# Moving the block for the expected head pattern out of a conditional, and the block for other patterns behind it

## The chip, the core and the metric

The kernel runs on one core of one Trainium2 chip. Its five engines work from queues of their own, in order, and meet at semaphores: TensorE (PE, matrix products; PEld stands for its weight loads), VectorE (DVE), ScalarE (ACT), GpSimd (POOL) and SyncE (SP), which here only issues transfers. The metric is the device time of one execution in microseconds.

## The reference

Two stages follow each other. The first is attention over 4 batches, 8 heads, 768 positions and 64 values per head; some heads ("retrieval") see all earlier positions, the others only 4 first positions and a window of 64:

```python
scores = scale * np.matmul(q, k.transpose(0, 1, 3, 2))
stream_keep = causal & (is_sink | in_win)
mask = np.where(retr[0, :, 0, 0, None, None], full_mask, stream_mask)
scores = np.where(mask[None, :, :, :], scores, -1000000000.0)
a = softmax(scores)              # written out in the original
x = np.matmul(a, v)              # heads joined: 4 x 768 x 512
```

The second is a gated circular convolution along the 768 positions, done with Fourier transforms:

```python
x1, x2, x3 = split(x @ w_proj, 3)
x2_conv = np.fft.irfft(np.fft.rfft(x2, axis=1) * np.fft.rfft(filter_fft, axis=0), n=S, axis=1)
out = (x1 * x2_conv * x3) @ w_out
```

Which heads are retrieval heads is an input, `is_retrieval`; it is 1, 0, 1, 0, 0, 0, 1, 0.

## The kernel before, in words

The kernel holds two complete programs for this. `patterned` is laid out for the expected pattern of heads and leaves out the blocks that the mask makes empty; `general` works for any pattern. Which one runs is decided on the chip: `lflag` (L1016) loads `is_retrieval`, four VectorE instructions (L1027 to L1030) compare it with the pattern and leave 0 or 1 in the tile `other`, every engine loads that value into a register (L1788) and branches on it (L1789).

Inside `patterned` every step is a named operation, and two strings of names give the order in which they are recorded. `AHEAD` is run before the branch, `FAST` in its else-block. A recording layer then gives each engine its queue; it works on one straight stretch of code at a time, and a branch ends a stretch. So in this kernel the instructions of `AHEAD` stand ahead of the branch on every engine and those of `FAST` behind it.

`AHEAD` holds: the load of the flag and of the first q and k blocks (`lflag lk0 lq0 lk1 lq1`, L1016, L1369); the comparison; and the start of the Fourier tables. The tables come out of a short chain: `tfrac` (L1080, VectorE), `turns` (L1133, ScalarE), then `angle`, `wrap`, `size` (L1137, L1141, L1146, VectorE), then `sin` and `cos` (L1151, L1155, ScalarE). Beside it `mtab0` and `mtab1` (L1096, VectorE, and L1100, GpSimd) start the mask table, and five matrix products on zeros (`blank0`, L1041) give TensorE something to do.

`FAST` begins with what the first attention blocks need. `ck0`, `cq0` (L971, VectorE) turn the loaded k and q to 16 bits; `T0.1`, `T0.0` (L1407) transpose them on TensorE; `E0.1`, `E0.0` (L971 on VectorE, L975 on ScalarE) copy the transposes out; `sc` (L1452) makes scores; `sb` (L1465) adds the mask as a product of the identity with a table `btab`; `ex` (L1471, ScalarE) takes the exponential. `btab` (L1129, VectorE) waits for the rest of the mask table, `mtab2` and `mtab3` (L1107 to L1125, GpSimd). Beside it the Fourier tables are finished from sine and cosine: `skew0` and `skew1` (L1163 on ScalarE, L1161 on GpSimd), the `G` tiles (L1161, L1188, L1201, L973), and `Gh` (L1214, VectorE). Later, per batch, come the projections (L1655, L1620), the spectra (L1620 to L1638), the inverse transform (L1685) and the output product (L1712), which is stored from L1732 and L1734.

The two blocks of the conditional lie one behind the other in the code of each engine, `FAST` first. An engine that ends `FAST` jumps over the whole of `general` (3517 instructions on PE) to a common end. There SP waits in turn for all transfers and all engines, the last for the last store, and then a barrier of all engines ends the program.

Of the kernel before, what the change touches and what calls it, by code (L numbers as in the profile page):

```python
# [9 lines left out]
FP32 = mybir.dt.float32  # L10
# [110 lines left out]
AHEAD = """  # L121
# [1632 lines left out]
@with_exitstack  # L1754
def kernel(
    ctx: ExitStack,
    tc: tile.TileContext,
    q: bass.AP,
    k: bass.AP,
    v: bass.AP,  # L1760
    is_retrieval: bass.AP,
    n_sink: bass.AP,
    window: bass.AP,
    moe_w_proj: bass.AP,
    moe_filter_fft: bass.AP,
    moe_w_out: bass.AP,
    out: bass.AP,
):
    nc = tc.nc
    H = q.shape[1]  # L1770
    assert H == 8 and int(window) <= 64 and int(n_sink) <= 64
    first = ctx.enter_context(tc.tile_pool(name="first", bufs=1))
    raw = {name: first.tile([128, size // 2], BF16, name="r_" + name) for name, size in RAW.items()}
    pools = {"raw": raw}
    raw["P0"] = raw["P"][:, 0:768]
    raw["P1"] = raw["P"][:, 768:2304]
    for name, size in (("mtab", 1792), ("other", 4), ("flag", 64), ("zeros", 64), ("local", 32), ("want", 32),
                       ("differs", 32)):
        raw[name] = first.tile([128, size // 2], BF16, name="r_" + name)
    run, held, left = patterned(tc, pools, None, q, k, v, is_retrieval, int(n_sink), int(window), moe_w_proj,  # L1780
                                moe_filter_fft, moe_w_out, out)
    engine = mybir.EngineType
    engines = {engine.Pool, engine.SP, engine.DVE, engine.PE, engine.Activation}
    with tc.tile_pool(name="bpsum", bufs=1, space=bass.MemoryType.PSUM) as psum:
        pools["space"] = psum.tile([128, 8, 512], FP32, name="bspace")
        with tc.manual_schedule(engines=engines):
            run(AHEAD)
    reg = nc.values_load(held["other"][0:1, 0:1], min_val=0, max_val=1)  # L1788
    with tc.If(reg != 0, preferred_fallthrough_block=False) as cmp:  # L1789
        general(tc, raw, q, k, v, is_retrieval, n_sink, window, moe_w_proj, moe_filter_fft, moe_w_out, out)  # L1790
    with cmp.Else(), ExitStack() as inner:
        inner.enter_context(tc.manual_schedule(engines=engines))
        pools["sb"] = inner.enter_context(tc.tile_pool(name="fsb", bufs=1))
        psum = inner.enter_context(tc.tile_pool(name="fpsum", bufs=1, space=bass.MemoryType.PSUM))
        pools["space"] = psum.tile([128, 8, 512], FP32, name="space")
        run(FAST)
    assert not left(), left()


# [33 lines left out]
```

## Time and profile before

| | |
|---|---|
| median of 3 runs | 190.54 us (190.18 to 191.35) |
| the profiled execution's own time | 190.34 us |
| its span in the profile | 188.6 us, so 1.74 us lie outside it |
| granted TensorE clock, mean | 0.985 |
| busy: PE, DVE, ACT, POOL | 176.5, 161.1, 145.7, 68.5 us |
| issues of the branch (L1789), first and last | POOL 3.6 us, SP 4.1, DVE 4.6, ACT 5.1; at the end ACT 182.6, SP 183.7 |

The span begins with the first instruction of the program and ends with its last barrier. An engine's busy time counts only work, not branches, register loads, waits or the issue of transfers; those show in the views of a line or of the waits. The chain of waits follows the work that ended last back to the start, from each piece to what released it.

### The profile page before, as it was taken

The page shows a single profiled execution, that of the slowest core. Times are in us where ns is not written, and L with a number is a line of the kernel's source. Part 1 is how long each engine was busy: PE and PEld are TensorE (multiplying, and loading weights), DVE is VectorE, ACT ScalarE, POOL GpSimd, SP SyncE. Part 2 cuts the span into 40 slices and gives each one's busy share as a digit, 9 for nine tenths or more (in the row PEclk, how much of TensorE's full clock was granted, in tenths as well). Part 3 has the DMA queues.
Part 4 walks back from the last instruction along what each step waited for, and adds up shares of the span by engine and source line. Part 5 has one row for each costly group of instructions (what it writes and reads, how often), then busy time and mean ns, then how long its engine had stood idle before and what let it go on. Part 6 is the DMA issues. An engine that isn't in the chain of part 4 may idle for free.

```text
span 188.6 us, 4479 instructions
## 1 busy us (share of the span) xinstructions
PE 176.5 (94%) x1694; PEld 103.5 (55%) x1694; DVE 161.1 (85%) x329; ACT 145.7 (77%) x210; POOL 68.5 (36%) x103
## 2 busy tenths in 40 slices
PE   6989999989998999999999999999999999999970
PEld 2446664647745563575555656655657765455420
DVE  6886799889979999999979999999899996499810
ACT  5887899999999999988989999696976331435350
POOL 5884785554322224570250450600741630000000
PEclk9988999999999999999999999999999999999997
DMA  4999999999999999999999989922262002412083
GB/s 161 332 270 283 206 196 239 271 292 240 219 198 229 210 210 171 218 220 194 231 244 254 217 250 225 214 47 50 82 76 111 3 2 113 146 24 111 37 299 126
DMA packets 78960, 34.06 MB, mean 181 GB/s; under 512 B 68306, under 2 KB 75218, under 8 KB 78930
## 3 DMA queue, kind: packets, MB, share of 16 engines
q1 hardware_dynamic: 75986, 30.81, 72.8%
q0 software_dynamic: 2944, 2.88, 9.1%
q8 instruction: 15, 0.25, 0.6%
q14 instruction: 15, 0.12, 0.3%
HBM read 24.64 MB, written 6.29 MB: 164 GB/s over the span
## 4 chain that ended last, share of the span: by engine, by line
PE 67%; ACT 14%; DVE 11%; issue 3%; POOL 2%; DVEq 0%; ACTq 0%; POOLq 0%
PE space L1655 19%; PE space L1712 11%; PE space L1620 8%; PE space L1452 7%; PE space L1685 7%; PE space L1516 6%; ACT f_pT L1471 5%; ACT f_HAB L1274 3%; PE space L1465 2%; PE space L1569 2%; DVE f_attn L1533 1%; PE space L1571 1%; ACT f_xh L975 1%; DVE r_P L978 1%; PE space L1407 1%
## 5 line engine op out<-in xcount | busy, mean ns | idle before, releaser
L1471 ACT ACTIVATE f_pT<-space 128x1024 bf16<-128x1024 f32 (+3 forms) x68 | 58.8, 917 | 6.3 <-PE space L1465 2.1
L1655 PE MATMUL space<-f_xT,f_wproj 128*128 128x384 bf16 x256 | 47.9, 326 | 0.1
L1655 PEld LDWEIGHTS <-f_wproj 128*128 128x128 bf16 x256 | 24.0, 98 | 17.0 <-issue 1.0
L1712 PE MATMUL space<-f_wout,r_gy 128*128 128x512 bf16 x96 | 24.7, 379 | 0.0
L1452 PE MATMUL space<-f_qkT 64*128 64x128 bf16 (+3 forms) x248 | 22.4, 252 | 1.2 <-DVE f_qkT L971 0.6
L1620 PE MATMUL space<-f_wproj,f_xh 128*128 128x512 bf16 x96 | 22.7, 379 | 0.1
L1685 PE MATMUL space<-f_Gi,r_P 128*128 128x384 bf16 x96 | 19.1, 326 | 0.6 <-ACT f_evs L975 0.3
L978 DVE TENSOR_TENSOR f_pT<-f_pT,r_mtab 128x1024 bf16<-128x1024 bf16 (+3 forms) x33 | 18.5, 585 | 1.0 <-ACT f_pT L1471 0.8
L975 ACT COPY f_o<-space 128x1024 f32<-128x1024 f32 (+1 forms) x12 | 9.9, 836 | 11.3 <-PE space L1712 11.2
L1516 PEld LDWEIGHTS <-f_pT 128*128 128x128 bf16 x472 | 16.6, 97 | 3.6 <-issue 0.9
L1516 PE MATMUL space<-f_v_aug,f_pT 128*128 128x65 bf16 x392 | 17.9, 193 | 0.6 <-ACT f_X L975 0.5
L978 POOL TENSOR_TENSOR f_uv<-f_fo 128x256 bf16<-128x256 bf16 x12 | 9.1, 765 | 23.3 <-DVE f_fo L978 19.0
L1452 PEld LDWEIGHTS <-f_qkT 64*128 64x128 bf16 x248 | 10.3, 94 | 13.1 <-issue 10.4
L1696 DVE TENSOR_TENSOR f_conv<-f_evs,space 128x384 bf16<-128x384 f32 x32 | 16.1, 547 | 0.6 <-PE space L1685 0.3
L975 ACT CAST f_xh<-space 128x768 bf16<-128x768 f32 x14 | 11.2, 808 | 4.9 <-PE space L1573 4.6
L1620 PEld LDWEIGHTS <-f_xh 128*128 128x128 bf16 x96 | 9.0, 97 | 10.0 <-issue 0.4
L1712 PEld LDWEIGHTS <-r_gy 128*128 128x128 bf16 x96 | 9.0, 98 | 8.9 <-issue 0.4
L1533 DVE TENSOR_TENSOR f_attn<-space,f_rec 128x768 bf16<-128x768 f32 x14 | 13.4, 955 | 0.4
L1685 PEld LDWEIGHTS <-r_P 128*128 128x128 bf16 x96 | 8.8, 97 | 7.3 <-DVE r_P L978 0.9
L978 POOL TENSOR_TENSOR f_fo<-f_attn 128x384 bf16<-128x384 bf16 x11 | 10.4, 957 | 2.4 <-DVE f_attn L1533 1.9
L975 ACT CAST f_X<-space 128x1024 bf16<-128x1024 f32 x8 | 8.2, 1019 | 2.8 <-PE space L1620 2.0
L978 POOL TENSOR_TENSOR f_pT<-f_pT,r_mtab 128x512 bf16<-128x512 bf16 (+1 forms) x6 | 6.7, 1117 | 9.5 <-ACT f_pT L1471 9.5
(136 smaller groups left out, 346.2 us busy)
## 6 DMA issues: line engine op xcount, KB each, us to landing
f_v_f<-in_v_dram SPq DMA_DIRECT2D x32, 192.0 KB, 4.8
out_dram<-f_o SPq DMA_DIRECT2D x9, 512.0 KB, 2.9
r_qk_f<-in_k_dram SPq DMA_DIRECT2D x10, 192.0 KB, 4.5
r_qk_f<-in_q_dram SPq DMA_DIRECT2D x10, 192.0 KB, 5.3
r_qk_f<-in_k_dram SPq DMA_DIRECT2D x4, 384.0 KB, 11.4
r_qk_f<-in_q_dram SPq DMA_DIRECT2D x4, 384.0 KB, 6.0
f_qk_f<-in_q_dram SPq DMA_DIRECT2D x4, 384.0 KB, 5.5
f_qk_f<-in_k_dram SPq DMA_DIRECT2D x4, 384.0 KB, 6.6
```

The costliest lines, as they stand in the source:

```text
L975: nc.scalar.copy(out=out, in_=in_)
L978: (nc.gpsimd if now["engine"] == "p" else nc.vector).tensor_tensor(out, a, b, op)
L1274: nc.scalar.activation(out=out_(), in_=in_(), func=AF.Copy, scale=w / S)
L1452: nc.tensor.matmul(sc[:, bank, col:col + 128 * cnt], lhsT=keys, rhs=qkT(n)[rows, 0, 128 * i:128 * (i + cnt)], start=(col == 0 or not biase ...
L1471: nc.scalar.activation(out=pT(n)[:, c, :, 0:w], in_=held[f"sc.{n}.{c}"][:, :, 0:w], func=AF.Exp, scale=SCALE)
L1516: nc.tensor.matmul(att[:, hh, 65 * i:65 * i + 65], lhsT=pT(n)[:, c, bank, col:col + 128], rhs=values, start=(z == 0), stop=(z == len(here) ...
L1533: nc.vector.tensor_mul(attn(n).rearrange("p i hh d -> p hh i d"), rows[:, :, :, 0:64], held[f"rec.{n}"][:, :, :, None].to_broadcast([128, ...
L1620: nc.tensor.matmul(ps[:, u, :], lhsT=xh(b)[:, cc, chain, 128 * part:128 * part + 128], rhs=wproj()[:, cc, DM:2 * DM], start=(cc == 0), sto ...
L1655: nc.tensor.matmul(ps[:, s, 0:HS], lhsT=wproj()[:, cc, part * DM + cb * 128:part * DM + (cb + 1) * 128], rhs=xT(b)[:, cc, s * HS:s * HS + HS],
L1685: nc.tensor.matmul(ps[:, 0, 0:HS], lhsT=P(b)[:, t, u, ch], rhs=Gi()[:, tile_no], start=(m == 0), stop=(m == 2))
L1696: fn(conv[:, half * HS:half * HS + HS], held[f"evs.{b}.{cb}"], held[f"c_ps.{b}.{cb}.1"][:, 0, 0:HS])
L1712: nc.tensor.matmul(ps, lhsT=gy(b)[:, cb, i * 128:(i + 1) * 128], rhs=wout()[:, cb, :], start=(cb == 0), stop=(cb == NC - 1))
```

## The change

`patterned`'s two parts now both stand in the straight code, ahead of the conditional; the test is done behind them; and only if the pattern is another one, `AHEAD` is run once more and then `general`, which overwrites the output. A hint at the very first instruction of every engine names the branch and says that it is likely taken (past the block).

```diff
-    run, held, left = patterned(tc, pools, None, q, k, v, ...)
+    def prepared():
+        return patterned(tc, pools, None, q, k, v, ...)
...
+    def ahead(run, name):
+        with tc.tile_pool(name=name, bufs=1, space=bass.MemoryType.PSUM) as psum:
+            pools["space"] = psum.tile([128, 8, 512], FP32, name="bspace")
+            with tc.manual_schedule(engines=engines):
+                run(AHEAD)
+
+    run, held, left = prepared()
+    tc.mark_branch_hint_location("other", "LikelyTaken", engines)
+    ahead(run, "bpsum")
     reg = nc.values_load(held["other"][0:1, 0:1], min_val=0, max_val=1)
-    with tc.If(reg != 0, preferred_fallthrough_block=False) as cmp:
-        general(tc, raw, q, k, v, ...)
-    with cmp.Else(), ExitStack() as inner:
+    with ExitStack() as inner:
         inner.enter_context(tc.manual_schedule(engines=engines))
...
         run(FAST)
     assert not left(), left()
+    with tc.If(reg != 0, label="other"):
+        ahead(prepared()[0], "apsum")
+        general(tc, raw, q, k, v, ...)
```

In the built program `AHEAD` and `FAST` are now one stretch, and the recording layer orders them as one. Past the first twenty instructions every engine's queue is what it was, up to the end. The start of VectorE's queue, before and after, by the names used above (`copy E0.1` is the copy out of the first transpose):

```
before: blank want table        tfrac quarter mtab0 zeros            local            differs reduce angle wrap size | branch | ck0 par cq0 copy-E0.1 | Gm00 btab ck1 Gm01 Gh0 ...
after:  blank want table   ck0  tfrac quarter mtab0 zeros  par  cq0  local copy-E0.1  differs reduce angle wrap size |                              | Gm00 btab ck1 Gm01 Gh0 ...
```

(`zeros`, `local`, `differs`, `reduce` are the four instructions that compare the flags.) `ck0` waits for the first load of k, `cq0` for that of q, the copy for the transposes. On GpSimd two memsets (L1353) stand ahead of L1089 and L1100, and L1120 to L1125 follow as before. ScalarE and TensorE keep their order and lose the load and the branch. SP issues the next transfers without the branch and loads `other` behind its tenth transfer; the other engines load it at the very end.

At the end each engine loads `other`, branches, and lands in a small block of its own, again past the whole of the other block. It holds what brings the semaphores to the same values that the other way would leave: on SP eight waits, one for each of the eight semaphores of transfers, the last of them for the last store. Behind it stands the common end as before, with SP's twelve waits and the barrier.

More of the change, by code (lines that the diff above doesn't have):

```diff
@@ L1779 @@
         raw[name] = first.tile([128, size // 2], BF16, name="r_" + name)
-    run, held, left = patterned(tc, pools, None, q, k, v, is_retrieval, int(n_sink), int(window), moe_w_proj,
-                                moe_filter_fft, moe_w_out, out)
+    def prepared():
+        return patterned(tc, pools, None, q, k, v, is_retrieval, int(n_sink), int(window), moe_w_proj,
+                         moe_filter_fft, moe_w_out, out)
     engine = mybir.EngineType
     engines = {engine.Pool, engine.SP, engine.DVE, engine.PE, engine.Activation}
[L1784 to L1787, printed above, removed]
+    def ahead(run, name):
[6 more added lines that the diff above has]
+    ahead(run, "bpsum")
     reg = nc.values_load(held["other"][0:1, 0:1], min_val=0, max_val=1)
-    with tc.If(reg != 0, preferred_fallthrough_block=False) as cmp:
-        general(tc, raw, q, k, v, is_retrieval, n_sink, window, moe_w_proj, moe_filter_fft, moe_w_out, out)
-    with cmp.Else(), ExitStack() as inner:
+    with ExitStack() as inner:
         inner.enter_context(tc.manual_schedule(engines=engines))
@@ L1797 @@
     assert not left(), left()
+    with tc.If(reg != 0, label="other"):
+        ahead(prepared()[0], "apsum")
+        general(tc, raw, q, k, v, is_retrieval, n_sink, window, moe_w_proj, moe_filter_fft, moe_w_out, out)
 _INS = ['q', 'k', 'v', 'is_retrieval', 'n_sink', 'window', 'moe_w_proj', 'moe_filter_fft', 'moe_w_out']
```

## The prediction

> **What bounds the kernel now.** I read the chain of waits first: on the page as shares, then piece by piece for the first 32 us, because the change touches the start.
>
> ```profile
> ## 4 chain that ended last, share of the span: by engine, by line
> PE 67%; ACT 14%; DVE 11%; issue 3%; POOL 2%; DVEq 0%; ACTq 0%; POOLq 0%
> ```
>
> No transfer is in it: what ends last is a chain of engine work from start to end, two thirds of it TensorE. Its first pieces (start us, us, what):
>
> ```profile
> 3.42 0.57 DVE r_gy L1141
> ...
> 4.01 0.57 DVE r_gy L1146
> ...
> 4.61 0.62 ACT r_P L1155
> ...
> 5.31 1.06 POOL f_skew L1161
> ...
> 7.17 0.52 POOL r_mtab L1113
> ...
> 7.78 1.04 POOL r_G L1161
> ...
> 9.29 0.67 DVE f_Gh L1214
> ...
> 11.03 0.88 DVE f_qkT L971
> ...
> 11.95 0.37 PE space L1452
> 12.32 0.53 PE space L1465 x4
> ```
>
> So the sine and cosine are on the path: `wrap`, `size`, `cos`, then GpSimd without a gap (skew, mask, G), VectorE without a gap from 9.29, scores at 11.95. Behind that each piece starts where the one before it ends. What delays 11.95 by some time delays the end by that time, as long as the pieces behind it keep their lengths. The register load and the branch are not in the chain: GpSimd has done with them at 3.6 us and waits for `cos` until 5.31.
>
> Then the branch's own line (min/median/max ns, first to last start us):
>
> ```profile
> L1789 PEldq COMPARE_BRANCH  x2: 90/2256/4422, 3.6 to 178.6; - x2
> L1789 SPq COMPARE_BRANCH  x2: 46/48/49, 4.1 to 183.7; - x2
> L1789 ACTq COMPARE_BRANCH  x2: 38/42/45, 5.1 to 182.6; - x2
> ```
>
> The branch at the start costs each engine 0.05 to 0.1 us behind a register load of 0.47 to 0.54 us (L1788). The jump at the end is far: 4.42 us on PE itself; on ScalarE the first instruction behind it (L1828) comes at 185.8, 3.2 us after the jump at 182.6; on VectorE 3.0.
>
> Last, the clock in stretches (length; PE, PEld, DVE, ACT, POOL busy with counts; PE clock, DMA share, GB/s):
>
> ```profile
> 8.90:12.30 3.40, 2.31 (x23) 0.99 (x22) 3.13 (x8) 3.07 (x4) 2.57 (x9) 1.00 1.18 299
> 12.30:15.70 3.40, 3.40 (x24) 2.21 (x24) 1.76 (x3) 3.03 (x4) 3.37 (x7) 0.50 1.29 227
> 15.70:19.10 3.40, 3.40 (x46) 2.30 (x44) 2.78 (x5) 2.03 (x3) 0.68 (x3) 1.00 1.01 324
> ```
>
> A stretch with PE busy 2.31 of 3.40 us is followed by one at half the clock.
>
> **1. The start: VectorE's new order (+5.2 us).** The removed branch saves nothing on the chain. But `ck0` now stands ahead of `tfrac`, and `par`, `cq0` and the copy of the transposes ahead of `angle`; a queue is in order, so the sine waits for the first load of k. I walk the queue with start-to-start steps from the timeline of the profile.
>
> - The first k block is issued at 1.23 and takes 3.2 us to land (the shortest of L1369's first landings): 4.4. SP's queue is the same up to there. `ck0` starts at 4.45 (0.05 from landing to start, as for GpSimd's cast at 10.93 after a landing at 10.88).
> - `ck0` to the next 0.52, `tfrac` to `quarter` 0.09, `quarter` to `mtab0` 0.19, `mtab0` to `zeros` 0.73, `zeros` to `par` 0.09, `par` to `cq0` 0.16, `cq0` to the next 0.62, `local` to the copy 0.13: the copy starts at 6.98. TensorE's transposes, released by `ck0` at 5.05, need 0.5 us: not late.
> - copy to the next 0.87, `differs` 0.19, `reduce` 0.08: `angle` at 8.12, against 2.90 now. Then 0.52 to `wrap`, 0.59 to `size`, 0.60 to `cos` at 9.83, 0.62 its length: 10.45, against 5.23.
>
> The chain goes on behind `cos` with the queues that it had: GpSimd's skew at 10.5, its last mask instruction to 12.9, `btab` behind that, G, `Gh`, the copy. VectorE's four pulled-up instructions are done, but it has nothing to do until ScalarE's skew at 10.9, and from `Gh` on it is released by GpSimd again. So 11.95 becomes 17.2: **+5.2**. ScalarE is shifted a little less: it follows `cos` with 0.4 + 0.5 + 1.28 + 0.2 + 0.4 us (skew, G, table load, two small ones), no longer waits 0.83 us for q at 8.71, and reaches the first exponential at 15.3 instead of 10.94, +4.3. That is the lower end of what the shift can be before the clock, since ScalarE is busy 19.8 of the 20 us from 30 to 50.
>
> The loads do not give it back: none is on the chain. SP issues its sixth transfer some 1.0 us sooner (4.20 now, behind 0.5 us of load, 0.2 of register work and the branch), and later stops for the register load until `reduce` is done (8.2, plus 0.7). Behind it is the load that it now issues at 8.75: no loss, with five transfers still to land.
>
> **2. The clock (-0.5 us, from -1.7 to +1.0).** TensorE has nothing between the last of its zero products (about 8.2) and the transposes of the second k block (13.9). By the rows above 12.3 to 15.7 is at half clock again, and, with PE at work in only half of it, I take 15.7 to 19.1 too. The products that ran at half clock at 12.3 to 15.7 now run at 17.5 to 20.9: the 1.8 us behind 19.1 need half, -0.9; those ahead of 17.5 are mostly hidden by GpSimd and VectorE, and I charge +0.4. Ends: all of the 3.4 us at full clock, -1.7; one half-clock stretch more, of which 1 us is not hidden, +1.0.
>
> [...]
>
> **3. The end: waits behind the last store (+0.86 us).** SP's waits at 184.2 to 184.8 follow each other at 0.07 us. Now most are done while stores fly, and the last one is that for the last store. In the changed program the new block waits for the last store first, and the common end's twelve waits come after: 12 x 0.072 = 0.86. That nothing of it is hidden follows from the order: the wait for the last store is SP's last in the new block.
>
> **4. The end: the far jumps (-0.65 us, from -1.3 to 0).** The jumps themselves are covered: ScalarE is done with its own at 185.8, the last store lands at 187.6, so 1.8 us of cover; the added register load (0.5 us) fits in it. But their code is fetched by the same DMA engines as the stores. The packets show a 16 KB fetch for PE at 184.1, 1.39 us long; of the last store's 16 parts fifteen have landed by 186.34 and one at 187.64. If the hint has the code brought in earlier, the last store lands up to 1.3 us sooner; if not, 0. No row shows a hint; I take the middle.
>
> [...]
>
> **Sum**, against the profiled execution's 190.34: 190.34 + 5.2 - 0.5 + 0.86 - 0.65 = **195.3 us**. That execution lies 0.2 under the median of 190.54, which I leave out.
>
> **The rivals.**
> - *The hint is spent* by the time of the branch: part 4 is 0, **195.9**. For it: 3398 PE instructions lie between, with a fetch of 16 KB about every 11 us. Against: a hint names its branch.
> - *The delay is partly caught up* at 12 to 22 us: ScalarE idles there 3.4 - 3.03, 3.4 - 2.03 and 3.4 - 2.85, together 2.3 us. If these waits are for something that now comes early, 5.2 becomes 2.9 and with parts 3 and 4 the time is **193.4**. Against: the chain in that stretch is TensorE back to back.
> - *The hint displaces code*: an engine stalls once for a fetch it did not need before. Price by the far jumps 3.0 to 4.4 on top of 195.3, **198.3 to 199.7**. Against: nothing here shows it.
> - *Not slower: loads bind the start.* If the first scores wait for k, q and v and not for the mask and tables, `cos` may come late for free, and SP's 1.0 us is a gain: 190.34 - 1.0 + 0.86 - 1.3 = **188.9**. It decides if the load is the later of the two at the first scores. For it: ScalarE's cast at 8.71 and GpSimd's at 10.93 do wait for transfers (0.83 and 0.72 us). Against: `cos` would end at 10.45 and `btab` at 13, behind both.
>
> **How the numbers follow.** Forecast 0.48, hint spent 0.30, caught up 0.10, hint displaces 0.08, not slower 0.04. Low end: all low ends, 190.34 + 5.2 - 1.7 + 0.86 - 1.3 = 193.4, which is also the caught-up case; high end: 190.34 + 5.2 + 1.0 + 0.86 = 197.4, and 198.2 to reach toward the displaced case, whose 8% stay out. A measurement of this kernel can tell about 1% (1.9 us) from no change. Slower by over that 0.93; within it 0.05 (a catch-up larger than 2.9, or part of the last rival); faster 0.02.
>
> **What would show it.** Step 1: `angle` near 8.1 and `cos` near 9.8 us; the scores that stand at 11.95 now near 17; VectorE idle from about 1.4 to 4.4 and again before 10.9. Step 2: half clock from 12 to 19. Step 3: a row of SP waits of about 0.9 us between the last landing and the barrier. Step 4: no 16 KB packet among the last stores. The prediction is wrong if `angle` starts before 4 us, if the shift at the first scores isn't found again at the end, or if engines stall in the middle.

## The result and the profile after

| | before | after |
|---|---|---|
| median | 190.54 us (190.18 to 191.35) | 196.24 us (195.30 to 196.97) |
| ratio, 95% interval | | 1.029 [1.025, 1.033] |
| profiled execution, its own time | 190.34 us | 196.97 us |
| its span | 188.6 us | 195.1 us |
| granted TensorE clock, mean | 0.985 | 0.972 |
| `angle` starts | 2.90 us | 8.38 us |
| `cos` starts | 4.61 us | 9.92 us |
| first scores on the chain | 11.95 us | 17.67 us |
| first product with an exponential (L1516) | 20.02 us | 26.97 us |
| ScalarE's last copy ends, to the end of the span | 5.41 us | 5.00 us |

The changed kernel is 2.9% slower; 195.3 was forecast. The profiled execution is the slowest of the changed kernel. So the same program was profiled a second time, on another chip (`changed_again` below): 195.34 us there, with a median of 195.56 us (195.22 to 196.15). Ratios leave out executions over 1.5% above the fastest of the same kernel, so they need not be the quotient of two medians.

The page of the changed kernel has the shares of the chain:

```profile
PE 65%; ACT 14%; DVE 10%; issue 3%; DMA 2%; POOL 2%; SPq 0%; DVEq 0%; ACTq 0%; POOLq 0%
```

A transfer is now in it (DMA 2%), where before there was none. The chain of waits, first 18 us of the changed kernel (start us, us, what), says which:

```profile
1.79 4.55 DMA r_qk_f<-in_q_dram
...
6.37 0.56 DVE f_qk_bf L971
6.93 0.40 DVE r_local L1028
7.33 0.87 DVE f_qkT L971
...
8.45 0.34 DVE r_gy L1137
...
8.90 0.57 DVE r_gy L1141
...
10.61 0.86 POOL f_skew L1161
...
15.58 0.83 DVE r_G L971
...
17.67 0.58 PE space L1452
```

`angle` (L1137) stands behind the cast of q and the copy of the transposes, and these behind a load. Everything from there to the scores is the old chain, later by 5.3 to 5.7 us. One piece is new: the cast of G at 15.58 was 0.2 us long on the chain and is now 0.83.

The clock, in stretches of the changed kernel (length; PE, PEld, DVE, ACT, POOL busy with counts; PE clock, DMA share, GB/s):

```profile
8.90:12.30 3.40, 0.20 (x1) 0.00 (x0) 1.34 (x3) 2.79 (x5) 1.56 (x4) 1.00 1.17 309
12.30:15.70 3.40, 1.86 (x16) 1.33 (x16) 2.60 (x6) 2.88 (x6) 3.32 (x8) 0.71 1.21 246
15.70:19.10 3.40, 2.76 (x17) 1.19 (x16) 2.85 (x5) 1.51 (x2) 2.23 (x6) 0.50 1.01 292
19.10:22.50 3.40, 3.40 (x25) 2.22 (x23) 1.18 (x2) 2.94 (x4) 2.25 (x4) 0.50 1.16 298
22.50:26.00 3.50, 3.50 (x38) 2.06 (x36) 2.99 (x5) 1.58 (x2) 1.20 (x2) 0.79 1.09 349
```

TensorE has next to nothing to do from 8.9 to 12.3 us (0.20 us), and then half the clock from 13.70 to 23.94: 10.2 us, three times the 3.4 us of before.

Last, the branch in the changed kernel (min/median/max ns, first to last start us):

```profile
L1804 PEldq COMPARE_BRANCH  x1: 390/390/390, 186.7 to 186.7; - x1
...
L1804 ACTq COMPARE_BRANCH  x1: 68/68/68, 190.2 to 190.2; - x1
```

PE's far jump took 4.42 us before; it takes 0.39 us now. The hint was given at 0.8 us, some 3400 PE instructions ahead of the branch; the run without it (4.40 us), below, shows that it did this.

From the first product with an exponential on, every ScalarE instruction of the changed kernel is 6.92 to 6.95 us later than before, to the last one. Nothing in the middle gives any of it back or adds to it. So the whole difference is made before 27 us and behind the last copy. In a budget against the profiled 190.34 us of before:

| | forecast | first execution | second execution |
|---|---|---|---|
| `cos` later (VectorE's order) | +5.2 | +5.31 | +4.77 |
| from `cos` to the first scores | 0 | +0.41 | +0.40 |
| from the scores to the first product (put down to the clock) | -0.5 | +1.23 | +0.15 |
| end: SP's waits behind the last landing | +0.86 | +0.74 | +0.74 |
| end: the last store's landing | -0.65 | -1.14 | -1.15 |
| time outside the span | 0 | +0.10 | +0.10 |
| sum (the time itself) | 195.3 | 196.99 (196.97) | 195.35 (195.34) |

### The profile page after: what moved, and what is told of

It is laid out like the page before. It is cut to its first block, busy times and chain, and to the rows that moved or that the text cites. A ratio compares the mean times of both kernels' runs of the same rounds, so it can differ in the third digit from the quotient of the medians.

```text
span 195.1 us, 4493 instructions
## 1 busy us (share of the span) xinstructions
PE 179.5 (92%) x1694; PEld 105.1 (54%) x1694; DVE 161.6 (83%) x329; ACT 145.5 (75%) x210; POOL 69.0 (35%) x103
## 4 chain that ended last, share of the span: by engine, by line
PE 65%; ACT 14%; DVE 10%; issue 3%; DMA 2%; POOL 2%; SPq 0%; DVEq 0%; ACTq 0%; POOLq 0%
PE space L1655 18%; PE space L1712 11%; PE space L1620 8%; PE space L1452 7%; PE space L1685 6%; PE space L1516 6%; ACT f_pT L1471 5%; ACT f_HAB L1274 2%; DMA r_qk_f<-in_q_dram 2%; PE space L1465 2%; PE space L1569 2%; DVE f_attn L1533 1%; PE space L1571 1%; ACT f_qk_bf L975 1%; PE space L1407 1%
## 5 line engine op out<-in xcount | busy, mean ns | idle before, releaser
L1452 PE MATMUL space<-f_qkT 64*128 64x128 bf16 (+3 forms) x248 | 23.5, 261 | 1.1 <-DVE f_qkT L971 0.6
L1516 PEld LDWEIGHTS <-f_pT 128*128 128x128 bf16 x472 | 16.6, 97 | 3.6 <-issue 0.9
L1516 PE MATMUL space<-f_v_aug,f_pT 128*128 128x65 bf16 x392 | 17.9, 193 | 0.6 <-ACT f_X L975 0.5
L1407 PE MATMUL space<-r_identity,f_qk_bf 128*128 128x128 bf16 x96 | 9.0, 248 | 4.7 <-DVE f_qk_bf L971 4.7
L1407 PEld LDWEIGHTS <-f_qk_bf 128*128 128x128 bf16 x96 | 7.3, 113 | 6.7 <-DVE f_qk_bf L971 5.2
```

The costliest lines, as they stand in the source:

```text
L1407: nc.tensor.transpose(ps[:, 0, t * 128:(t + 1) * 128], qk_bf(n)[:, a, t].rearrange("p hh d -> p (hh d)"), identity())
L1452: nc.tensor.matmul(sc[:, bank, col:col + 128 * cnt], lhsT=keys, rhs=qkT(n)[rows, 0, 128 * i:128 * (i + cnt)], start=(col == 0 or not biase ...
L1516: nc.tensor.matmul(att[:, hh, 65 * i:65 * i + 65], lhsT=pT(n)[:, c, bank, col:col + 128], rhs=values, start=(z == 0), stop=(z == len(here) ...
```

## Experiments

The theory was: the order of VectorE's first instructions makes nearly all of the loss; the straight code and the hint by themselves cost nothing in the middle; the end is a small gain less a small loss.

**The same program again.** No edit: the changed kernel on another chip, as the yardstick for what follows.

> The changed kernel itself, on one chip with the runs below. Theory: 195.3 to 197, with little spread, since behind a late start no load is waited for; the kernel before spreads more, where loads and tables are about equally late.

195.56 us (195.22 to 196.15), ratio 1.025 [1.020, 1.030]. The spread is small, as expected: 0.93 us, against 2.55 us of the kernel before on the same chip (189.52 to 192.07). In its profile k landed at 4.49 us and q at 5.63, which nothing waited for; `angle` starts at 7.84 (8.12 was forecast). In the first execution q landed at 6.35, and `cq0` waited for it until 6.37 instead of 6.08; `local` behind it then took 0.48 us instead of 0.25, beside a GpSimd instruction (L1120) that ended at 7.31, 0.02 us ahead of it. These two make the 0.54 us between the two values of `angle`. So two loads can hold the sine up: k in both profiled executions, q in one of them. The half clock lasts 14.14 to 20.97 here, two lengths of 3.41 us and not three. Over both sets, the executions with a mean clock of 0.970 to 0.972 took 195.78 to 196.97 us and those with 0.976 to 0.978 took 195.22 to 195.80. If the lower clock stands for a third length, as it does in the two profiled ones, a third length costs 0.7 to 1.0 us.

**The straight code with the old order.** `AHEAD` and `FAST` are recorded in one schedule with one PSUM tile, which gives VectorE its old order; the load of `other`, the conditional behind and the hint stay.

```diff
-    ahead(run, "bpsum")
-    reg = nc.values_load(held["other"][0:1, 0:1], min_val=0, max_val=1)
     with ExitStack() as inner:
...
+        run(AHEAD)
+        pools["sb"] = inner.enter_context(tc.tile_pool(name="fsb", bufs=1))
         run(FAST)
+    reg = nc.values_load(held["other"][0:1, 0:1], min_val=0, max_val=1)
```

> The changed kernel, but AHEAD and FAST recorded under one schedule, so that VectorE's queue has its old order (tfrac to size ahead of ck0, par, cq0 and the copy); code still straight, hint and conditional block as changed. Theory (the order at the start costs 5.3 us, the idle TensorE behind it another 0 to 1.2, the end gives 0.4 back): all but the end is undone, cos near 4.7 us, first 512-wide score product near 12.0, clock 0.985, time 189.6 to 190.6. Rival (straight code, its hint or code fetches cost time in the middle): stays at 194 or more.

191.11 us (189.19 to 192.61), ratio 0.998 [0.993, 1.002]: the whole loss is gone, though the median lies above the 189.6 to 190.6 that were expected. The chain of waits of this kernel, to be read against that of before (4.61, 5.31, 11.95):

```profile
4.34 0.52 ACT r_P L1151
4.86 0.52 ACT r_P L1155
...
5.46 1.06 POOL f_skew L1161
...
10.64 0.20 DVE r_G L971
...
12.10 0.58 PE space L1452
```

The scores come 0.15 us later than before, not 5.7, and PE's jump takes 385 ns. (The profiled execution took 192.37 us, more than the median; it loses more behind the scores, with half clock from 11.54 to 18.37 us.) So neither the conditional behind, nor the hint, nor the straight code costs anything that can be measured: the order does.

**One instruction moved.** As the last, but `ck0` alone put ahead of `tfrac`.

```diff
-        run(AHEAD)
+        run(AHEAD.replace("tfrac", "ck0/v tfrac"))
...
-... blank10@1 ck0/v skew0/s ...
+... blank10@1 skew0/s ...
```

> Straight code, hint, old order but for one instruction: ck0 alone stands ahead of tfrac; par, cq0 and the copy stay behind size. Theory (a queue in order: the wait for the first k load goes to all that stands behind): angle at 6.6 to 6.7, cos at 8.3 to 8.4 us, so 3.7 of the 5.3 us from this one instruction; time 193.5 to 195.3. Rival (only the four together, by their length, make the delay; the load's wait alone is small): cos before 6 us, under 192.5.

195.05 us (194.64 to 195.65), ratio 1.022 [1.017, 1.027]. The chain of waits of this kernel:

```profile
1.32 4.31 DMA r_qk_f<-in_k_dram
...
5.66 0.56 DVE f_qk_bf L971
6.22 0.06 DVE r_tfrac L1080
...
7.82 0.58 DVE r_gy L1137
...
10.22 0.86 POOL f_skew L1161
```

The transfer, the cast, `tfrac`, and `angle` at 7.75: the one cast in front of the tables makes some 3.9 us of loss by the medians (191.11 to 195.05, on two chips), 4.6 by the ratios, of 4.5 to 5.3 in all. But `angle` was expected at 6.6 to 6.7. In this execution the load of k took 4.32 us to land, and in the other eleven profiles 3.16 to 3.32, so this profile shows the wait some 1.1 us longer than usual. What `par`, `cq0` and the copy add in the changed kernel isn't settled: on one chip the two kernels are 0.5 us apart (195.05 and 195.56), with intervals that overlap.

**The hint taken out**, from the changed kernel and from the straight kernel with the old order.

```diff
-    tc.mark_branch_hint_location("other", "LikelyTaken", engines)
```

> The changed kernel without the hint. Theory (the hint keeps the fetches of the far jump out of the last stores): jumps of 3 to 4 us on PE, VectorE and ScalarE again, last store 3.9 to 4.4 us from issue to landing, time 0.4 to 1.1 us above the changed kernel. Rival (the last store lands as early without the hint; only jumps that are covered anyway change): within 0.3 us.

> The run above without the hint. Theory (the hint has the code at the far end of the jump brought in early, so that no fetch stands in the way of the last stores): far jumps of 3 to 4 us on PE, VectorE and ScalarE come back, a fetch of 16 KB among the last stores, last store 4.4 us from issue to landing in place of 3.3; 0.5 to 1.1 us slower than with the hint, 190.5 to 191.3. [...]

The changed kernel without its hint: 196.15 us (195.65 to 197.17), ratio 1.028 [1.023, 1.034], on the chip of the second set (195.56 there). The line of the branch in it:

```profile
L1803 PEldq COMPARE_BRANCH  x1: 4397/4397/4397, 185.6 to 185.6; - x1
```

The far jump is back, with fetches of 16 KB (on queue q8, which is read here as PE's) at 187.51 and 190.74 us, and the stretch from ScalarE's last copy to the end of the span is 5.36 us against 4.98. So the hint is worth 0.38 us by the profiles; by the medians it is 0.6, with intervals that overlap. But the last store doesn't land late again, as the 3.9 to 4.4 us of the theory had it. The landing of the last store alone (L1732): before, changed, changed without the hint.

```profile
DMA to landing us min/median/max: 4.4/4.4/4.4
```

```profile
DMA to landing us min/median/max: 3.3/3.3/3.3
```

```profile
DMA to landing us min/median/max: 3.4/3.4/3.4
```

To the hundredth these are 4.40, 3.26 and 3.41 us. So 0.99 of the 1.14 us that the landing gained is there without the hint, and the hint adds 0.15; the rest of what it is worth lies between the landing and the end of the span (1.92 us without it, 1.71 with it). What made the 0.99 stays open. One thing that differs from before is that PE now loads `other` for 1.08 us ahead of its jump, so that its second fetch starts 1.62 us behind the issue of the last store and not 0.87 us; no run tests this by itself.

The straight kernel without the hint took 191.46 us (189.43 to 192.59), ratio 1.001 [0.997, 1.005]: no difference from the one with it that can be measured, where 0.5 to 1.1 us were expected, and its last store lands in 3.22 us (3.49 with the hint), not in 4.4. Its profile, of an execution of 192.31 us, shows something else. It runs at full clock to 188 us and has its first product with an exponential at 19.27 us, 0.75 ahead of before; yet it ends later than before. The chain of waits of this execution says why:

```profile
16.15 6.07 DMA f_qk_f<-in_q_dram
...
26.61 17.05 DMA r_qk_f<-in_k_dram
...
48.00 5.22 DMA f_HAB<-f_HAB
```

With its early start, transfers end last further on; a lead of 0.75 us has become a lag of 1.95 us at ScalarE's last copy. One execution, 0.85 us over the median, proves little, but the kernel without the conditional, next, does the same. So before looks close to two bounds, the tables and the transfers. A late start has slack in the second; that would be why the loss goes through rigidly and a gain doesn't.

**Without the conditional.** Only the expected pattern: the load of `other`, the branch, the hint and the block for other patterns are left out.

```diff
-    with tc.If(reg != 0, label="other"):
-        ahead(prepared()[0], "apsum")
-        general(tc, raw, q, k, v, ...)
```

> The program for the expected pattern alone, straight, old order at the start: register load, branch, hint and the block for other patterns are left out, so it is right for the expected pattern only. Theory: without the serial waits behind the last store (0.74 us) and without a jump, 0.6 to 1.0 us under the first run, 188.8 to 189.8. Rival (the conditional at the end costs nothing that the barrier wouldn't take anyway): the same as the first run.

189.49 us (188.22 to 190.79), ratio 0.990 [0.984, 0.995]; it is 1.6 us under the first run, more than the 0.6 to 1.0 expected. From the last copy to the end of the span it takes 2.98 us, not 5.00 (after) or 5.41 (before); its last store lands 2.03 us after its issue, not 3.26 (after) or 4.40 (before). The packets from 175 us to the end, by queue (packets, MB, share); first of the changed kernel, which ends later and so has more data in that stretch, then of this one:

```profile
q1 hardware_dynamic: 1408, 2.62, 28.0%
q14 instruction: 3, 0.02, 0.3%
q8 instruction: 1, 0.02, 0.2%
```

```profile
q1 hardware_dynamic: 1234, 2.27, 24.0%
```

Without a jump nothing fetches code there, and the last 24 packets of the stores end within 0.13 us of each other. In the changed kernel the last nine of 2 KB trail one by one at 0.08 us, from 192.43 to 193.06 us. The 2.4 us that the end gains on before are lost in the middle of the profiled execution (190.79 us, 1.3 over the median): ScalarE is 1.07 us ahead of before at 21.5 us and 2.61 us behind at 34.5. A length of half clock (26.89 to 30.30 us) lies in there, and the chain has this piece just ahead of it:

```profile
15.88 10.14 DMA f_qk_f<-in_q_dram
```

**The jump at the start, hinted.** The kernel before with its blocks exchanged, `general` first, so that the far jump falls to the branch at the start, and the hint at the first instruction.

```diff
+    tc.mark_branch_hint_location("other", "LikelyTaken", engines)
...
-    with tc.If(reg != 0, preferred_fallthrough_block=False) as cmp:
+    with tc.If(reg != 0, preferred_fallthrough_block=True, label="other") as cmp:
```

> The kernel before with the block for other patterns laid ahead of that for the expected one, and the hint at the first instruction for the branch at 3 to 5 us, which is now the far jump; no jump is left at the end and no waits are added behind the last store. Theory (a hint two or three us ahead is enough, and fetches beside the last stores cost about 1 us): start as in the kernel before within 0.3 us, last store 3.0 to 3.4 us from issue to landing, 0.5 to 1.2 us faster than before. Rival (the fetch comes too late at the start): a stall of up to 3 us at the branch on every engine, 1 to 3 us slower than before.

194.15 us (192.11 to 195.17), ratio 1.013 [1.006, 1.019]. The line of the branch in it:

```profile
L1790 PEldq COMPARE_BRANCH  x1: 6581/6581/6581, 3.7 to 3.7; - x1
```

Its stretches (columns as above):

```profile
4.80:9.60 4.80, 0.00 (x0) 0.00 (x0) 0.00 (x0) 0.33 (x1) 1.15 (x5) 1.00 1.00 319
```

The hint stood 3 us ahead of the branch and didn't cover the jump: PE waits 6.6 us, VectorE 4.8, with the DMA engines at a share of 1.00, and PE's fetch starts only at 7.86 us. The end, free of jumps, takes 3.04 us, and its last store too lands in 2.03. So where the hint had the whole program ahead of the branch the jump was covered, and where it had 3 us it was not. What this branch would cost without a hint wasn't run.

**TensorE kept busy.** The changed kernel, with the fourth group of zero products longer, over the gap from 8.9 to 12.3 us.

```diff
-BLANKS = (5, 2, 2, 2, 2, 2, 2, 2, 2, 2, 2, 2, 2)
+BLANKS = (5, 2, 2, 26, 2, 2, 2, 2, 2, 2, 2, 2, 2)
```

> The changed kernel with 26 products on zeros in place of 2 behind the transposes of the first q block (about 5.6 us at full clock), so that TensorE isn't idle from 8.9 to 13.8 us; VectorE's order as changed. Theory (idle TensorE costs 1.2 us by half clock behind the late start): no half clock at 13.7 to 23.9, time 1.2 to 2.5 us under the changed kernel, 193.7 to 195.0. Rival (the clock is most of the loss): under 192. Rival (the clock is hidden behind the other engines): no change, 196.

195.68 us (195.24 to 195.99), ratio 1.024 [1.019, 1.029]: no gain over the changed kernel's 195.56, against what was expected. Its stretches (columns as above):

```profile
8.90:12.30 3.40, 3.35 (x16) 1.57 (x16) 0.87 (x3) 3.25 (x7) 2.03 (x4) 1.00 1.15 299
12.30:15.70 3.40, 2.95 (x26) 1.31 (x25) 3.06 (x7) 3.33 (x5) 3.31 (x8) 1.00 1.00 219
15.70:19.10 3.40, 2.13 (x19) 1.28 (x19) 3.17 (x6) 1.63 (x3) 2.29 (x8) 0.82 0.98 283
```

The busy TensorE kept its clock until 17.87 us, and one length of half clock followed, behind a stretch in which it was again busy for half (14.46 to 17.87: 1.69 of 3.41 us). The first product with an exponential comes only 0.31 us ahead of the changed kernel's (25.05 against 25.36), and 0.05 of that is left at the last copy. Until 19 us the products wait for VectorE's and GpSimd's tables, so a slow TensorE costs little there. That the third length costs more fits with its place (20.53 to 23.94), where TensorE is busy for all of the 3.41 us; that was not tried by itself.

**A cast moved from GpSimd to ScalarE.** The budget has +0.4 us between `cos` and the scores that the forecast did not have. In the order string of the changed kernel the cast of the third k block changes its engine.

```diff
-... E1.1/v sc0.1@4 sb0.1 lq6 ck2/p
+... E1.1/v sc0.1@4 sb0.1 lq6 ck2/s
```

> The changed kernel, with one piece moved: the cast of the third k block (ck2) goes from GpSimd to ScalarE, which idles there. Nothing is left out. In the changed kernel VectorE's cast of G at about 15.5 us lies beside GpSimd's cast of that block and takes 0.91 us, against 0.28 us before, where GpSimd was idle. Theory A (the two casts slow each other): VectorE's cast takes 0.28 to 0.5 us, the first scores come 0.4 to 0.6 us sooner than 17.1 to 17.7, and the span is that much shorter: 194.7 to 195.2 against 195.2 to 195.6 for the changed kernel. Theory B (the cast is long for another reason, such as its own operands): it still takes 0.9 us, and the time stays at 195.2 to 196.1. If ScalarE lacks the 0.6 to 1.0 us that its cast takes, the time rises by up to 0.5 us in both.

195.12 us (194.88 to 195.59), ratio 1.024 [1.018, 1.029]. The timeline of the changed kernel (second execution; start us, us, engine, line) around VectorE's cast of G:

```profile
14.71 1.02 POOL L973 CAST f_qk_bf<-f_qk_f 128x768 bf16<-128x768 f32 x1
14.97 0.91 DVE L971 CAST r_G<-r_P 128x256 bf16<-128x256 f32 x1
...
16.13 0.94 DVE L971 COPY f_qkT<-space 128x768 bf16<-128x768 bf16 x1
```

The timeline of the kernel with the cast moved:

```profile
14.98 0.28 DVE L971 CAST r_G<-r_P 128x256 bf16<-128x256 f32 x1
...
15.52 0.94 DVE L971 COPY f_qkT<-space 128x768 bf16<-128x768 bf16 x1
```

With GpSimd's cast gone, VectorE's takes 0.28 us, as before the change, and the copy that the scores wait for starts 0.61 us sooner. The first product with an exponential gains 0.75 us; 0.35 of it goes again near 117 us, behind a transfer (L1645), and 0.40 is left in the profiled time (194.94 against 195.34). The intervals of the two ratios overlap, so the gain in time isn't shown by itself; the lengths of the cast are. The two casts get in each other's way: VectorE's takes 0.91 us beside GpSimd's and 0.28 without it. In the kernel before GpSimd's cast waited for its load until 10.93 us, just behind VectorE's (10.41, 0.28 long); 5 us later the load has long landed, and the wait that kept them apart is gone. VectorE's cast ends at 15.88, 0.15 us behind the end of GpSimd's at 15.73, and GpSimd's is longer too (1.02 us against 0.83). How the one holds the other up is not shown.

**A filled start on the old order.** The straight kernel with the old order, with a few more zero products near 8 to 13 us, to see if it can beat the kernel before.

```diff
-BLANKS = (5, 2, 2, 2, 2, 2, 2, 2, 2, 2, 2, 2, 2)
+BLANKS = (5, 2, 2, 3, 2, 2, 2, 2, 2, 2, 2, 2, 2, 1, 2)
...
-... lq4 T1.1@1 Gm01 ... E1.0/v sc0.4@0 ...
+... lq4 T1.1@1 blank13@0 Gm01 ... E1.0/v blank14@0 sc0.4@0 ...
```

> The straight kernel with the pieces in the order of the kernel before (191.11 us), with three groups of TensorE's zero products more or longer between 8 and 13 us, where TensorE otherwise has little to do. Nothing is left out. Theory A (a TensorE with little to do is followed by the half clock, and the half clock costs): the half-clock stretch of 3.4 to 6.8 us near 12 us goes, the first exponential comes 0.5 to 1 us sooner, and the time is 190.0 to 190.8 where the loads bind little. Theory B (loads take back what an earlier start gains): the stretch goes, the waits for the loads of q and k between 20 and 50 us grow by as much, and the time is that of the kernel before, 190.5 to 191.5. If the added products stand ahead of work that is waited for, up to 0.5 us slower.

191.14 us (189.73 to 192.74), ratio 0.999 [0.996, 1.003]: no difference. The half clock did not go in the profiled execution either (11.39 to 14.80), and a load of q that landed at 9.95 us took the place of the tables on its chain, so theory B has the result, but not a test of its own. No version that handles every pattern was found to be faster than the kernel before.

## Why the prediction was right, point by point

- **Bound.** The start is on the path, and what delays the scores delays the end: right. Each ScalarE instruction behind 27 us is later by the same 6.94 us (5.32 in the second execution). What the reading missed is that transfers bind almost as closely, which shows only in kernels that start early. For this change, which makes the start late, it made no difference.
- **Step 1, +5.2: right**, 5.31 and 4.77 by `cos`. Walked through the queue, `angle` came out at 8.12; it starts at 8.38 and 7.84. Three terms in it were off by some tenths. The walk had no wait for the load of q, and `local` at its short length; in the first execution q ended a wait (`cq0` at 6.37, 6.23 by the walk) and `local` was 0.23 us longer. And "the chain goes on behind `cos` with the queues that it had" left out that a wait had vanished from one of them, GpSimd's, so that its cast fell on VectorE's: +0.4, shown by the kernel with that cast moved.
- **Step 2, -0.5: wrong in sign**; +1.23 and +0.15. The step that failed is "the 1.8 us behind 19.1 need half". The half clock was put at 12.3 to 19.1 and came at 14.1 to 21.0 or 13.7 to 23.9, so the products from 19.1 on did not get the full clock that the gain was made of. The first of these is outside the range from -1.7 to +1.0 that was given. In these two executions of one program the stretches of half clock begin at 13.70 and 14.14 us and last 10.24 and 6.83 us, three times and twice 3.41.
- **Step 3, +0.86:** 0.74 (twelve waits at 0.062 us instead of 0.072); right.
- **Step 4, -0.65:** -1.14; right in sign and inside its range, but not by the mechanism given. The prediction took the middle between nothing and 1.3 us, not knowing if the hint works, and let all of the gain come from the hint. The hint does work on the jump (4.40 to 0.39 us). Yet the last store lands in 3.41 us without it, so 0.99 of the 1.14 us has another cause, which stays open; that the size came near is luck. And 3.26 us of landing are not the floor: both ends without a far jump land in 2.03. The packets that are left beside the stores (one of 16 KB, three of 8 KB) are the likely cause of the 1.2 us between; that was not tried by itself.
- **The rivals.** *Hint spent:* refuted by the jump of 0.39 us. Between a fetch of 16 KB for PE at 173.36 us (0.96 long) and the jump at 186.68 the trace has none, so the target seems to have been there some 12 us ahead of it. *Partly caught up:* refuted, the shift is rigid. *Hint displaces code:* refuted; no engine stalls, and the straight kernel with the hint costs nothing that can be measured. *Loads bind the start:* refuted for this kernel; a load does bind it, but ahead of the sine, where it costs.
- **The number.** 195.3 was forecast and 196.24 is the median, 195.56 in the second set. In the first set three of five executions have the lower mean clock, 0.972, and the median is one of them; in the second, three of six have 0.970 or 0.971. The forecast is near the others (195.22 to 195.80). That the second execution's 195.34 meets it almost exactly is luck in part: of its terms, the sine, the waits and the landing came out 1.05 us lower than forecast, and the cast, the clock and the time outside the span 1.15 us higher.

## What to carry to other kernels

When a branch goes, ask what order it had enforced: on an in-order queue one early cast that waits for a transfer can hold up a chain that needs no transfer, and here that cost some 4 us while the branch itself had cost nothing on the path. After working out a shift, look at the waits that it removes on neighbouring engines, since a wait can be what keeps two instructions from slowing each other (VectorE's cast, 0.28 us before and 0.91 after). And a lag can go through to the end in full, as the 6.94 us here did, where a lead is taken back by the next bound, as the 0.75 us of the straight kernel without the hint were.

## What the runs showed of the hardware that was not expected

- A branch hint at the first instruction still worked some 3400 PE instructions later (0.39 us for the jump, against 4.40 without it), while one 3 us ahead of its branch, with the DMA engines at a share of 1.00, left a stall of 6.58 us.
- An end of the program without far jumps is 2.0 to 2.4 us shorter: the last store lands in 2.03 us instead of 4.40 (before) or 3.26 (changed, where the waits behind it make the other 0.8 us). In the kernels with a far jump at the end, instruction fetches of 16 and 8 KB lie among the last stores.
- A VectorE cast of 0.28 us took 0.91 us beside a GpSimd cast, and GpSimd's took 1.02 us instead of 0.83.
